# Loads of x in smaller pieces with a limit on those in flight, a shorter chain to the band matrix, and a new order of work

## The chip, the cores and the metric

The kernel runs on one core of a Trainium2 chip. The metric is the device time of one execution in microseconds. Its engines are named as the profile does: PE (TensorE, matrix products; PEld is its loading of weights), ACT (ScalarE), DVE (VectorE), POOL (GpSimd) and SP (SyncE). PE writes its results to PSUM, eight banks of 512 float32 columns on 128 partitions. ACT and DVE move results from PSUM to SBUF. POOL and SP issue transfers (DMAs) between DRAM and SBUF here, which sixteen DMA engines carry out.

## The reference

The input x has 8 batches of 4224 tokens with 192 channels. A causal convolution over 7 tokens comes first, with one softmax-normalised filter for each of 8 heads of 24 channels. A token-mixing layer follows:

```
w   = softmax(weight, axis=-1)                        # [8 heads, 7 taps]
y   = sum over k of w[h, k] * x_pad[b, s + k, h, :]   # x_pad: 6 zero rows ahead of x
W   = (y @ w_q) @ (y @ w_k).T / sqrt(64)              # [b, 4224, 4224]
out = relu(W @ y) @ w_out
```

The kernel never forms W. It computes the 192 x 192 matrix G = y.T y per batch, makes M = w_k.T G from it, and then relu((y w_q) M / 8) w_out.

## The kernel before

Tokens are cut into 35 chunks of 122. Each is held in SBUF as 128 rows, its own 122 and the 6 ahead of it, so that a convolution is one matmul per head with a 128 x 128 band matrix, `BAND`. x is loaded by POOL, cast to bf16 on the way, into `XW`, which has room for all 8 batches. A load therefore never waits for space.

Per batch the work is: convolution of groups of chunks (`gen_conv`, L636), evacuated to `Y` (L671); transposes of Y (L395/L396 through a helper, and L726), evacuated to `YTL` and `YTH` (L698, L733); the product with w_q (L751, L755) to `WQT` (L771); the Gram matrix (L787); the small product M (`gen_mix_weights`); then, a batch later, the mixing matmuls (L878, L890), a relu (L907 on ACT, L908 on DVE), the product with w_out (L935, and L391/L392 through the helper `halves`), evacuation to `OUT` (L970) and a store by SP (L978).

A DMA from DRAM to `XW` carries rows of 192 channels, 384 bytes each once they are bf16. Batch 0 is loaded in four groups of 9 or 8 chunks; every later batch in two, of 18 and 17. The first chunk of a batch (no rows ahead of it) and the last (a short one) have small DMAs of their own. The DMAs of a group share a semaphore, and the group's convolutions wait for it.

Ahead of the first convolution stands a chain: an identity (POOL), a step matrix made from it (DVE L435), its transpose (PE, ACT L445), the softmax on small tiles (DVE L461 to L494 with one exponential on ACT, L482), matmuls that spread the taps (`spread`, L508), and two evacuations that make `BAND` (L527), one on ACT and one on DVE. DVE also clears several tiles in that time, in program order with the chain: `WQH`, `WKT`, `WKB`, `YTH`, `WQT`, `MBD` (L417, L419, L420, L411, L410, L422).

Nothing in the source fixes the order of the rest. Every step is an `Op` with assumed costs, what it needs, what it must follow (`after`, order only) and a turn. `Planner.plan` (L143) places the ops one by one: on each engine, of the ops that could start, the one with the lowest turn goes first. The turns come from the table `TURNS`, one number per op in the order in which the ops are made. PE ops have a mode (64 output rows from 128 input rows, or the other way); a change of mode costs `SWITCH` in the plan and `STAY` is added to the turn of an op that would change it. `HOLD` is how many ns PE may wait for an op of the mode it is in. The plan also chooses ACT or DVE for most evacuations, and PSUM banks. `Program` then gives each engine its list in that order, with semaphore waits where one engine needs another. The engines execute their lists in order.

Of the kernel before, what the change touches and what calls it, by code (L numbers as in the profile page):

```python
# [13 lines left out]
    int(t) / 1000  # L14
    for t in """
# [56 lines left out]
class Op:  # L72


    n = 0
# [28 lines left out]
class Planner:  # L104
# [6 lines left out]
    STAY = 0.865  # L111

    HOLD = 1
# [166 lines left out]
def bass_lightweight_conv__then__hypermixer_token_mlp_kernel(  # L280
# [25 lines left out]
    t = 0  # L306
# [67 lines left out]
    def bank(i, n=1):  # L374
        return PS[:, i * 512 : (i + n) * 512]

    def add(*a, dma=None, kind=None, **k):
        op = Op(*a, **k)
        op.dma = dma
        op.kind = kind  # L380
        op.vt = TURNS[len(planner.ops)]
        return planner.add(op)
# [11 lines left out]
    def turn_halves(e, out, in_, identity):  # L394
# [34 lines left out]
        1250,  # L429
# [28 lines left out]
        200, needs=[ident], vt=-8.92)  # L458
# [44 lines left out]


    bands = []
    for q0, engine in ((0, "ACT"), (4, "DVE")):

        def spread(e, op, q0=q0):  # L508
            last = None
            for q in range(q0, q0 + 4):  # L510
                last = halves(
                    e,
                    bank(op.bank)[:, (q - q0) * 128 : (q - q0 + 1) * 128],
                    STEPT[0:112, 112 - 16 * q : 240 - 16 * q],
                    TAPS[0:112, :, :].rearrange("p i h -> p (i h)"),
                    start=q == q0,
                    stop=q == q0 + 3,
                    skip_group_check=True,
                )
            return last  # L520

        fill = add("PE", spread, 260, needs=[taps, stept], banks=1, vt=-7 + 0.1 * q0)

        def band(e, op, q0=q0, fill=fill):
            dst = BAND[:, :, 16 * q0 : 16 * q0 + 64]
            src = bank(fill.bank).rearrange("p (j h) -> p h j", h=H)
            return e.copy(dst, src) if op.engine == "ACT" else e.tensor_copy(dst, src)  # L527

        bands.append(add(engine, band, 550, drains=fill, vt=-6.9))
# [3 lines left out]
    at = [5000.0]  # L533

    def gen_load(b, gi):
        sem = semaphore(f"s_x{b}_{gi}")
# [4 lines left out]
        if cs[0] == 0:  # L541
            parts.append((XW[KC - 1 : 128, b, 0, :], bass.AP(x_t, base, [[D, CW], [1, D]])))
        n = len(full)
        parts.append(
            (
                XW[:, b, full[0] : full[0] + n, :],
                bass.AP(x_t, base + (CW * full[0] - KC + 1) * D, [[D, 128], [CW * D, n], [1, D]]),
            )
        )
# [9 lines left out]
        at[0] += len(cs) * 260.0  # L559
        load[b, gi] = []  # L560
        for k, part in enumerate(parts):
            first = (b, gi) == (0, 0) and part[0].shape[1] > 1 and len(part[0].shape) == 3
            op = add(
# [3 lines left out]
                needs=[zero_x] if cs[-1] == NCC - 1 else [],  # L567
                after=[] if first else [ident],
                dma=(f"x{b}_{gi}", sem, 16),
                vt=-10 if first else -4 + b + gi * 0.1 + 0.02 * k,  # L570
            )
            op.tail = 1500.0
            op.lands = at[0]
# [485 lines left out]
```

## Time and profile before

| | us |
|---|---|
| median of 3 runs | 177.69 |
| lowest, highest | 177.29, 178.58 |
| the profiled execution | 177.53 |
| its span, first to last instruction | 175.7 |

In the page, x3226 is a number of instructions; a share is of the span. The parts that matter besides the lines shown with the prediction:

```profile
## 2 busy tenths in 40 slices
PE   0289799888999999899989979999999999999990
...
POOL 7999452524230000000000000000000000000000
...
DMA  3999999999999999999999999067283045987787
GB/s 30 162 189 186 205 191 193 191 196 277 193 279 194 286 309 268 343 250 243 304 264 282 237 194 348 24 244 297 103 343 127 4 175 216 356 347 309 265 303 262
```

Each slice is 4.4 us long; a digit is the busy share in tenths. The DMA row is full up to slice 24, some 105 us: in that time the loads of x run, with the stores of results among them from slice 8 on. After it only stores are left. In slices 2 to 8 loads run alone, at some 190 GB/s, counted in bytes that land.

```profile
q0 software_dynamic: 36128, 13.61, 65.1%
q1 hardware_dynamic: 12000, 26.31, 40.9%
...
out_dram<-out_sb SPq DMA_DIRECT2D x28, 768.0 KB, 5.1
xw<-in_x_dram POOLq DMA_DIRECT2D x7, 816.0 KB, 33.2
```

q0 are the loads of x that POOL issues (packets, MB, share of 16 engines' time); q1 the weights and the stores that SP issues. The last two lines give, for a group of DMAs, the KB of each and the median time from issue to landing. The seven large loads of 17 chunks take 33.2 us because they are issued long before their turn comes in the queue.

### The profile page before, as it was taken

The numbers are of one execution on the slowest core, as the hardware profiler recorded it, in microseconds if no ns is written. First come the engines' busy times: TensorE is split into PE (matmuls) and PEld (weight loads), VectorE is DVE, ScalarE is ACT, GpSimd is POOL, SyncE is SP. The second block draws the span as 40 slices with busy tenths as digits, with TensorE's granted clock in tenths as the row PEclk, the third lists the DMA queues.
The fourth block names the chain that finished last, engine by engine and source line by source line (L and its number), as shares of the span: only waits on it lengthen the run. The fifth ranks groups of instructions, "written<-read, shape, count | busy, mean of one in ns | idle before, by whom it ended". The sixth has DMA issues, their size and how long they took to land.

```text
span 175.7 us, 7099 instructions
## 1 busy us (share of the span) xinstructions
PE 157.1 (89%) x3226; PEld 121.7 (69%) x3226; DVE 118.0 (67%) x216; ACT 123.5 (70%) x206; POOL 30.3 (17%) x39
## 2 busy tenths in 40 slices
PE   0289799888999999899989979999999999999990
PEld 0179666776787787668778766878767777877550
DVE  6556587765766677586787738689688675765740
ACT  3243677597787948668648747888888896698980
POOL 7999452524230000000000000000000000000000
PEclk9999999999999999999999999999999999999995
DMA  3999999999999999999999999067283045987787
GB/s 30 162 189 186 205 191 193 191 196 277 193 279 194 286 309 268 343 250 243 304 264 282 237 194 348 24 244 297 103 343 127 4 175 216 356 347 309 265 303 262
DMA packets 48157, 40.36 MB, mean 230 GB/s; under 512 B 37632, under 2 KB 40960, under 8 KB 48128
## 3 DMA queue, kind: packets, MB, share of 16 engines
q0 software_dynamic: 36128, 13.61, 65.1%
q1 hardware_dynamic: 12000, 26.31, 40.9%
q8 instruction: 25, 0.41, 0.9%
q14 instruction: 4, 0.03, 0.1%
HBM read 27.56 MB, written 25.95 MB: 305 GB/s over the span
## 4 chain that ended last, share of the span: by engine, by line
PE 88%; issue 4%; DVE 3%; ACT 2%
PE ps L391 25%; PE ps L787 14%; PE ps L935 8%; PE ps L392 7%; PE ps L395 6%; PE ps L726 6%; PE ps L878 5%; PE ps L751 4%; PE ps L890 4%; PE ps L755 4%; PE ps L396 3%; ACT rt L907 1%; ACT out_sb L970 1%; DVE band L527 0%; DVE xw L416 0%
## 5 line engine op out<-in xcount | busy, mean ns | idle before, releaser
L970 ACT COPY out_sb<-ps 128x768 f32<-128x768 f32 (+1 forms) x46 | 34.7, 768 | 15.1 <-PE ps L392 11.3
L671 ACT CAST y<-ps 122x816 bf16<-122x816 f32 (+3 forms) x46 | 35.7, 791 | 13.2 <-PE ps L392 12.8
L907 ACT ACTIVATE rt<-ps 128x1024 bf16<-128x1024 f32 (+3 forms) x44 | 34.1, 800 | 6.4 <-PE ps L878 4.5
L787 PE MATMUL ps<-y 122*64 122x192 bf16 (+4 forms) x840 | 33.8, 222 | 2.2 <-issue 2.2
L970 DVE COPY out_sb<-ps 128x768 f32<-128x768 f32 (+1 forms) x26 | 21.6, 840 | 19.7 <-PE ps L392 18.5
L392 PE MATMUL ps<-wol,rt 128*64 128x192 bf16 x264 | 33.9, 255 | 1.0 <-issue 1.0
L787 PEld LDWEIGHTS ps<-y 122*64 122x64 bf16 (+1 forms) x840 | 31.1, 112 | 4.9 <-issue 2.8
L565 POOL DMA_DIRECT2D xw<-in_x_dram x34 | 29.9, 893 | 22.3 <-issue 21.5
L391 PE MATMUL ps<-wol,rt 128*64 128x192 bf16 x264 | 33.7, 255 | 0.0
L391 PE MATMUL ps<-xw,band 128*64 128x432 bf16 (+3 forms) x144 | 31.8, 335 | 1.5 <-DVE band L527 0.9
L392 PE MATMUL ps<-xw,band 128*64 128x432 bf16 (+3 forms) x144 | 32.1, 337 | 1.1 <-issue 1.1
L391 PEld LDWEIGHTS ps<-wol,rt 128*64 128x64 bf16 x264 | 24.1, 138 | 8.1 <-issue 2.0
L908 DVE TENSOR_SCALAR rt<-ps 128x512 bf16<-128x512 f32 (+3 forms) x36 | 23.6, 674 | 8.2 <-PE ps L878 7.6
L671 DVE CAST y<-ps 122x864 bf16<-122x864 f32 (+3 forms) x26 | 23.6, 912 | 8.0 <-PE ps L392 7.5
L698 DVE COPY ytl<-ps 128x976 bf16<-128x976 bf16 (+1 forms) x40 | 23.0, 591 | 3.9 <-PE ps L396 3.3
L392 PEld LDWEIGHTS ps<-wol,rt 128*64 128x64 bf16 x264 | 24.1, 138 | 1.2 <-issue 1.2
L396 PE MATMUL ps<-ident,y 122*64 122x122 bf16 x280 | 21.1, 219 | 0.0
L395 PE MATMUL ps<-ident,y 122*64 122x122 bf16 x280 | 21.0, 219 | 0.0
L935 PE MATMUL ps<-woh,rt 64*128 64x192 bf16 x264 | 20.4, 250 | 0.2 <-ACT rt L907 0.2
L395 PEld LDWEIGHTS ps<-ident,y 122*64 122x64 bf16 x280 | 18.1, 112 | 2.0 <-issue 0.5
L726 PE MATMUL ps<-ident,y 122*64 122x122 bf16 (+1 forms) x344 | 17.1, 220 | 1.3 <-DVE y L671 0.7
L396 PEld LDWEIGHTS ps<-ident,y 122*64 122x64 bf16 x280 | 17.7, 112 | 0.0
(95 smaller groups left out, 218.8 us busy)
## 6 DMA issues: line engine op xcount, KB each, us to landing
out_dram<-out_sb SPq DMA_DIRECT2D x28, 768.0 KB, 5.1
xw<-in_x_dram POOLq DMA_DIRECT2D x7, 816.0 KB, 33.2
xw<-in_x_dram POOLq DMA_DIRECT2D x7, 768.0 KB, 33.7
out_dram<-out_sb SPq DMA_DIRECT2D x8, 384.0 KB, 3.3
xw<-in_x_dram POOLq DMA_DIRECT2D x2, 432.0 KB, 8.3
out_dram<-out_sb SPq DMA_DIRECT2D x8, 96.0 KB, 4.3
xw<-in_x_dram POOLq DMA_DIRECT2D x1, 384.0 KB, 5.2
xw<-in_x_dram POOLq DMA_DIRECT2D x8, 45.8 KB, 25.0
```

Source lines behind the costliest of these rows:

```text
L391: e.matmul(out[0:64], lhsT[:, 0:64], rhs, **k)
L392: return e.matmul(out[64:128], lhsT[:, 64:128], rhs, **k)
L395: e.transpose(out[0:64], in_[:, 0:64], identity)
L396: return e.transpose(out[64:128], in_[:, 64:128], identity)
L565: lambda e, op, part=part: e.dma_start(*part),
L671: return e.copy(dst, src) if op.engine == "ACT" else e.tensor_copy(dst, src)
L726: last = e.transpose(ps[64 * i : 64 * i + HI, o : o + w], Y[0:w, yb, c, LO:D], IDENT[0:w, 0:w])
L787: mm = e.matmul(bank(GB)[p : p + 64, o : o + z - r], Y[0:w, yb, c, r : r + 64], Y[0:w, yb, c, r:z], start=st, stop=end, skip_group_check=True,
L907: return e.activation(dst, src(), AF.Relu)
L908: return e.tensor_scalar(dst, src(), 0.0, None, op0=ALU.max)
L935: last = e.matmul(bank(op.bank + a)[:, o : o + D], RT[64 * a : 64 * a + HI, slot, 2, i:n:nt], WOH[64 * a : 64 * a + HI, :], start=i == q, ...
L970: return e.copy(dst, src) if op.engine == "ACT" else e.tensor_copy(dst, src)
```

## The change

Loads: for b >= 1 the full chunks of a group go in four DMAs of 4 or 5 chunks each instead of one. Every DMA has a semaphore of its own. Each load of b >= 1, small ones too, waits until the third of the large loads ahead of it has landed. The assumed landing times of batch 0 are changed, and the assumed tail of a later load is 3200 ns.

```diff
+    big_loads = []
+    LANDS = [6000.0, 9900.0, 12300.0, 13900.0]
...
+        pieces = 4 if b else 1
+        for k in range(pieces):
+            some = full[len(full) * k // pieces : len(full) * (k + 1) // pieces]
+            parts.append(
+                (
+                    XW[:, b, some[0] : some[0] + len(some), :],
+                    bass.AP(x_t, base + (CW * some[0] - KC + 1) * D, [[D, 128], [CW * D, len(some)], [1, D]]),
+                )
             )
...
+            gate = big_loads[-3:][:1] if b else []
             op = add(
                 "POOL",
                 lambda e, op, part=part: e.dma_start(*part),
                 900,
-                needs=[zero_x] if cs[-1] == NCC - 1 else [],
+                needs=[*([zero_x] if cs[-1] == NCC - 1 else []), *gate],
                 after=[] if first else [ident],
-                dma=(f"x{b}_{gi}", sem, 16),
+                dma=(f"x{b}_{gi}_{k}", semaphore(f"s_x{b}_{gi}_{k}"), 16),
...
-            op.tail = 1500.0
-            op.lands = at[0]
+            op.tail = 1500.0 if b == 0 else 3200.0
+            op.lands = LANDS[gi] if b == 0 else 0.0
+            if len(part[0].shape) == 3:
+                big_loads.append(op)
```

Start: six clears are ordered behind the last step of the softmax (`taps`), `own` gets a later turn, and the band is spread and copied in four parts, two on ACT and two on DVE, instead of two.

```diff
+    for zero in (zero_w, zero_q, zero_yt, *zero_k, zero_m):
+        zero.after.append(taps)
...
-    for q0, engine in ((0, "ACT"), (4, "DVE")):
+    for q0, engine in ((0, "ACT"), (2, "DVE"), (4, "ACT"), (6, "DVE")):
...
-            dst = BAND[:, :, 16 * q0 : 16 * q0 + 64]
-            src = bank(fill.bank).rearrange("p (j h) -> p h j", h=H)
+            dst = BAND[:, :, 16 * q0 : 16 * q0 + 32]
+            src = bank(fill.bank)[:, 0 : 32 * H].rearrange("p (j h) -> p h j", h=H)
```

Order: all numbers of `TURNS` are new (two more ops for the band and 42 more for the loads are among them), and the planner's constants change.

```diff
-    STAY = 0.865
-    HOLD = 1
+    STAY = 0.909457
+    HOLD = 46.721672
```

The built orders show what comes of it. PE has the same matmuls in a new order. In the new one the convolutions of a batch's two halves stand further from each other in the early batches, and those of batch 7 stand earlier, after 2320 and 2344 of PE's 3226 matmuls instead of 2518 and 2448 for the second and first half. A convolution's first matmul waits for two to four semaphores of x instead of one. POOL has 76 loads instead of 34. On DVE the six clears stand between the taps and the first band copy. ACT has 38 large output copies instead of 43, DVE 26 instead of 21.

More of the change, by code (lines that the diff above doesn't have):

```diff
@@ L13 @@
 TURNS = [
-    int(t) / 1000
+    int(t) / 1e6
     for t in """
[50 rows of a table removed]
[84 rows of a table added]
 """.split()
@@ L428, in bass_lightweight_conv__then__hypermixer_token_mlp_kernel @@
         ),
-        1250,
+        700,
         needs=[one],
@@ L457, in bass_lightweight_conv__then__hypermixer_token_mlp_kernel @@
         lambda e, op: e.tensor_reduce(OWN[:, :], IDENT[:, :].rearrange("p (k i) -> p i k", i=16), AX.X, ALU.add),
-        200, needs=[ident], vt=-8.92)
+        200, needs=[ident], vt=-7.83)
     mx = add("DVE", lambda e, op: e.tensor_reduce(WMX[:, :], WT_F[:, :, :], AX.X, ALU.max), 150, needs=[load_w], vt=-8)
@@ L502, in bass_lightweight_conv__then__hypermixer_token_mlp_kernel @@
     taps.needs.append(own)
+    for zero in (zero_w, zero_q, zero_yt, *zero_k, zero_m):
+        zero.after.append(taps)
     bands = []
-    for q0, engine in ((0, "ACT"), (4, "DVE")):
+    for q0, engine in ((0, "ACT"), (2, "DVE"), (4, "ACT"), (6, "DVE")):
         def spread(e, op, q0=q0):
             last = None
-            for q in range(q0, q0 + 4):
+            for q in range(q0, q0 + 2):
                 last = halves(
@@ L516, in spread @@
                     start=q == q0,
-                    stop=q == q0 + 3,
+                    stop=q == q0 + 1,
                     skip_group_check=True,
@@ L520, in spread @@
             return last
-        fill = add("PE", spread, 260, needs=[taps, stept], banks=1, vt=-7 + 0.1 * q0)
+        fill = add("PE", spread, 200, needs=[taps, stept], banks=1, vt=-7 + 0.1 * q0)
         def band(e, op, q0=q0, fill=fill):
-            dst = BAND[:, :, 16 * q0 : 16 * q0 + 64]
-            src = bank(fill.bank).rearrange("p (j h) -> p h j", h=H)
+            dst = BAND[:, :, 16 * q0 : 16 * q0 + 32]
+            src = bank(fill.bank)[:, 0 : 32 * H].rearrange("p (j h) -> p h j", h=H)
             return e.copy(dst, src) if op.engine == "ACT" else e.tensor_copy(dst, src)
-        bands.append(add(engine, band, 550, drains=fill, vt=-6.9))
+        bands.append(add(engine, band, 340, drains=fill, vt=-6.9))
     load = {}
-    at = [5000.0]
+    big_loads = []
+    LANDS = [6000.0, 9900.0, 12300.0, 13900.0]
     def gen_load(b, gi):
-        sem = semaphore(f"s_x{b}_{gi}")
         cs = groups_of(b)[gi]
@@ L542, in gen_load @@
             parts.append((XW[KC - 1 : 128, b, 0, :], bass.AP(x_t, base, [[D, CW], [1, D]])))
[L543 to L547, printed above, removed]
+        pieces = 4 if b else 1
[6 more added lines that the diff above has]
+                )
             )
-        )
         if cs[-1] == NCC - 1:
@@ L557, in gen_load @@
             )
-        at[0] += len(cs) * 260.0
         load[b, gi] = []
```

134 rows, old and new, of the table TURNS are left out of this document.

## The prediction

> **What bounds the kernel now.** I read the engine shares first, then PE in stretches, then each place where PE stands still.
>
> ```profile
> span 175.7 us, 7099 instructions
> ...
> PE 157.1 (89%) x3226; PEld 121.7 (69%) x3226; DVE 118.0 (67%) x216; ACT 123.5 (70%) x206; POOL 30.3 (17%) x39
> ...
> q8 instruction: 25, 0.41, 0.9%
> ```
>
> PE is busy 157.1 of 175.7 us, ACT and DVE 70 and 67%: PE is the bound, and a gain must come from the 18.6 us in which it is idle. The stretches (stretch, its length, PE busy and its matmuls, then PEld, DVE, ACT, POOL, the clock, the DMA share) place them:
>
> ```profile
> 80.00:100.00 20.00, 19.41 (x436) 15.65 (x435) 14.29 (x26) 13.78 (x26) 0.00 (x0) 1.00 1.39 257
> ...
> 120.00:140.00 20.00, 20.00 (x434) 15.44 (x430) 15.57 (x24) 16.81 (x28) 0.00 (x0) 1.00 0.43 165
> ```
>
> From 120 to 140 us PE never rests, and the stretch to 160 us reads 20.00 too. While the loads of x run (the last lands at 106.0 us; the DMA share is 1.3 to 1.6) it does. The other idle times are the start, 8.7 us until the first convolution, and the end, 4.8 us of evacuation and store after the last matmul. The timeline of PE shows all stops over 0.3 us after 12 us:
>
> ```profile
> 20.48 0.35 PE L787 MATMUL ps<-y 122*64 122x192 bf16 x5 [1.28 <-issue]
> ...
> 33.15 0.19 PE L726 MATMUL ps<-ident,y 76*64 76x76 bf16 x1 [0.50 <-issue]
> ...
> 40.15 0.33 PE L392 MATMUL ps<-xw,band 128*64 128x408 bf16 x1 [1.07 <-issue]
> ...
> 70.96 0.30 PE L787 MATMUL ps<-y 122*64 122x64 bf16 x4 [0.90 <-issue]
> ...
> 90.19 0.34 PE L391 MATMUL ps<-xw,band 128*64 128x432 bf16 x1 [0.59 <-issue]
> ...
> 103.09 0.30 PE L392 MATMUL ps<-wol,rt 128*64 128x192 bf16 x1 [0.99 <-issue]
> ```
>
> Together 5.33 us, and "issue" means that PE waited for nothing shown; two stand between the two halves of one L391/L392 pair, where the program has no wait. The DMA packets name the cause. Queue q8 moves 25 packets of 16 KB. Before each stop one of them ends 1.4 to 1.5 us before PE goes on: 18.96, 31.72, 38.66, 69.60, 88.72 and 101.67 us. Counted in PE's records, the first instructions after the stops are numbers 449, 961, 1217, 2497, 3265 and 3777: steps of whole multiples of 256, and 16 KB / 256 is 64 bytes. PE runs out of program. From the passing of one such boundary to the start of the next packet took 3.3 to 4.5 us for the 14 packets up to 103 us (mean 3.8), then 0 to 2.7 us (mean 1.3). With 0.95 us for the packet and 1.42 us after it a page arrives some 6.2 us after the boundary; PE uses one up in about 6. So through the whole load phase PE runs on the edge of its program supply. Stores show the same delay: 768 KB landed in 7 to 10 us during the loads and in 3.4 to 5.2 us after them.
>
> **The change, part by part.** Sums are against the profiled execution, 177.53 us: span 175.7 and 1.8 around it. The median of the runs, 177.69, lies 0.16 higher.
>
> *Pieces and gate.* Each half-batch load of b >= 1 (16 or 17 chunks) becomes four of 4 or 5 chunks, each issued when the third large load ahead has landed: at most three, some 600 KB, in flight, where the old kernel has up to seven large loads (816 KB) issued and not landed. On POOL behind the waiting instruction stand only later loads. POOL executes 42 more issues; the trace has 0.55 us for a one-chunk load, 0.98 for 7 chunks and 1.28 for 17, so about 0.85 us each and some 65 us in all on an engine that is otherwise idle. DVE does not feel them: its 128x976 copy takes 660 ns both while POOL issues (10 to 53 us) and after (661).
> What it buys is the wait of 3.8 us before each program packet. A piece has 4 x 128 / 16 = 32 rows per DMA engine. A gated piece is not at once there: POOL's issue (0.85) and the start of its packets come first, in which the two others are served, 1.03 us each at the 190 GB/s of the store-free slices. So a packet that arrives should find about one piece, 1 to 2 us, ahead of it. Page latency is then 1.5 + 0.95 + 1.42, about 4 us, under the 6 that PE needs, and the stops go. Bounds: 0 (the wait stays) and -6 (the six stops, and small ones at the other eight boundaries). By rate: 1653 matmuls between 20.5 and 103.1 us are 20.0 per us; at the 21.2 of 103 to 160 us they take 4.6 us less. I take -5.0, between the rate and the stops. What is late next is PE's own work.
>
> *The start.*
>
> ```profile
> 3.42 0.12 DVE L435 COPY step<-ident 128x128 bf16<-128x128 bf16 x1
> ...
> 4.70 0.15 DVE L461 TENSOR_REDUCE wmx<-wt_f 128x8 f32<-128x56 f32 x1
> ...
> 7.93 0.69 DVE L527 CAST band<-ps 128x512 bf16<-128x512 f32 x1 [1.16 <-PE ps L392]
> ```
>
> Six memsets leave the chain: three start from 3.02 on, ahead of the step copy (3.42), three from 4.28 on, ahead of wmx (4.70); 0.8 us in all. The identity is there at 2.70, DVE free at 2.94, so the step copy starts near 3.04 (-0.4) and wmx at 3.9; the weights landed at 3.75, so they just do not bind. The taps end at 5.96 instead of 6.76, PE starts at 6.02. The six memsets (0.82) now stand between taps and bands on DVE, 6.03 to 6.85; its first band's fill is done at 6.65, so 0.2 us of them show. A quarter of the band (256 columns) costs about 0.42 us on DVE (0.69 for 512, 0.29 for a 128-column cast from PSUM) and 0.38 on ACT: bands end near 7.7 instead of 8.62. First convolution -0.9; the first x landed by 6.8, so it does not bind. It carries through if later loads are in time: the fourth group's landing, 15.1 us, is 2.3 ahead of its convolution. Between -0.2 and -1.2; I take -0.9.
>
> *The order.* PE's instructions are the same; the built orders have 97 changes between 64-row and 128-row matmuls instead of 107. At the end of the trace one such change delays the next matmul by 0.05 to 0.09 us: 10 x 0.07 = -0.7 (0 to -1.4). Waits on x grow from 18 to 52, each extra one an instruction of 51 ns on PE's sequencer; in the trace those lie beside the running matmul nearly everywhere, so +0.3 of a possible 1.7. Evacuations shift from ACT to DVE (five output copies, 0.80 against 0.96 us, and five 512-column relus), with three casts the other way: both stay near 70%, +0. The tail keeps its form: eight 384 KB stores and a last one of 96 KB, 0.
>
> Sum: -5.0 - 0.9 - 0.7 + 0.3 = -6.3, so 171.2 in a profiled execution and **171.4 us** as the median.
>
> **Rivals.**
>
> *The fetch waits as before.* Its wait was the same, 3.3 to 4.5 us, with seven large loads queued (18 us) and with the last two (97 us), so it may hang on there being any load at all. The sum without -5.0 is 176.4 us. Against it: a piece holds 32 rows per engine, the old loads 136, and gated pieces leave gaps. The Trainium skill says so outright ("DMA: Bandwidth & Descriptors", section "Queues, rings and completion order"): each engine goes round the queues packet by packet, so a shorter backlog in one queue would not shorten the wait of another. The trace's constant wait agrees with that; whether the packets of a small piece are shorter no run shows. Chance 0.14.
>
> *The loads starve.* The weights' 28 KB took 2.95 us from issue to landing; with 1.03 us of data a piece takes 4.0 us, so three make 147 GB/s, 23% under the 190 of before. Under stores the loads made only 100 GB/s even with a full queue, so there the limit of three costs little. Need and landing: in the new order the first half of batch 1 comes after 310 matmuls instead of 308, so it is needed at 23.5 - 1.28 - 0.9 = 21.3 us, and by my chain (issues at 11.4, 13.2, 15.1 and 16.4) lands at 20; the second half of batch 5 comes after 1628 matmuls, which the trace reached at 90.7, so it is due near 85.5 (stops up to there and the start taken off) and landed at 77.1 before; batch 7 comes after 2320, at 124.0, so it is due near 118 and landed by 106.0. Counted from 21.3, the old landing of its first group, the loads may be 14% slower. At 23% throughout, batch 7 comes at 125.5, 7.6 us late: 179 us, slower than before. It decides from 21% on (6.3 us late). The Trainium skill speaks for this ("DMA: Bandwidth & Descriptors", section "Bandwidth"): DMAs should be batched to 1 MiB or more. Chance 0.10.
>
> *The new order stalls PE elsewhere.* 303 PE instructions wait instead of 293, and convolutions move. From 160 to 165 us PE idles 0.18 us in 5 on evacuations; at that density over 140 us it is +5.0: 176.4. Against it, 120 to 160 us shows none. Chance 0.10.
>
> **Numbers.** The forecast has 0.62, its own range 169 to 174.5; a better order still, under 169, 0.04. A change under 1%, 1.8 us, can't be told from none in such runs, so "faster" ends at 175.9. The two rivals at 176.4 count mostly as the same; their milder halves (some stops left) still as faster: faster 0.75, same 0.15, slower 0.10. Range 169.0 to 177.0: it leaves out starved loads and part of the lucky side.
>
> **What would show it.** Right: no "issue" stops on PE between 18 and 105 us, program packets starting within 2 us of their boundary, stores landing sooner during the loads, a first convolution near 7.9 us, PE near 21 matmuls per us throughout, batch 7 landed before 118 us. Wrong: PE waiting for an x load in front of a convolution, stops at multiples of 256 instructions still there, or PE idle behind evacuations in the stretches that were full.

## The result, and the profile after

| | before | after |
|---|---|---|
| median, us | 178.09 (4 runs, 177.29 to 178.58) | 197.44 (4 runs, 196.07 to 198.78) |
| the profiled execution, us | 177.53 | 197.81 |
| its span, us | 175.7 | 196.1 |
| large loads all landed, us | 106.0 | 140.9 |

The ratio is 1.109 (95% interval 1.100 to 1.118): slower, where 171.4 us was forecast. The ratios below leave out executions well above the rest, among them the profiled ones of e9 and e13 (823.5 and 223.7 us), whose traces are not read; where that matters, the whole spread is given.

The chain that ended last, by engine, in the kernel before:

```profile
PE 88%; issue 4%; DVE 3%; ACT 2%
```

The page of the changed kernel, its shares, its clock, the same chain by engine and by line, and the loads' row:

```profile
span 196.1 us, 7150 instructions
...
PE 164.2 (84%) x3226; PEld 127.6 (65%) x3226; DVE 123.7 (63%) x219; ACT 120.6 (62%) x205; POOL 55.9 (29%) x81
...
PEclk9999999999969999999589999999559999999998
...
DMA 62%; PE 22%; POOL 8%; issue 4%; ACT 1%; DVE 0%; POOLq 0%; DVEq 0%
DMA xw<-in_x_dram 60%; POOL xw L606 8%; PE ps L425 6%; PE ps L978 3%; PE ps L830 3%; DMA out_dram<-out_sb 2%; PE ps L921 2%; PE ps L429 2%; PE ps L426 1%; PE ps L933 1%; PE ps L794 1%; PE ps L798 1%; PE ps L769 1%; ACT rt L950 1%; PE ps L430 0%
...
xw<-in_x_dram POOLq DMA_DIRECT2D x49, 192.0 KB, 5.5
```

PE was the bound before, with 88% of the chain; now 60% of it is loads of x, and another 8% their issue. PE is idle for 32 us instead of 18.6, and its clock, full until the tail before, falls to half three times. POOL's waits say which loads (line waited for, us in total, times, longest):

```profile
POOL xw L606 <- DMA xw<-in_x_dram: 80.2, 42, 5.2
```

42 of the 70 loads of b >= 1 had to wait, 80 us in all, of the 127 us between the first of these loads (issued at 11.6 us) and the last (138.9). All stops of PE over 0.4 us after 12 us, from its timeline:

```profile
14.87 0.24 PE L429 MATMUL ps<-ident,y 122*64 122x122 bf16 x1 [0.85 <-ACT y L714]
...
22.85 0.34 PE L425 MATMUL ps<-xw,band 128*64 128x432 bf16 x1 [0.62 <-DVE ytl L741]
...
36.88 0.34 PE L425 MATMUL ps<-xw,band 128*64 128x432 bf16 x1 [0.45 <-DMA xw<-in_x_dram]
...
54.16 0.34 PE L425 MATMUL ps<-xw,band 128*64 128x432 bf16 x1 [4.79 <-DMA xw<-in_x_dram]
...
75.75 0.32 PE L978 MATMUL ps<-woh,rt 64*128 64x192 bf16 x3 [0.48 <-issue]
...
93.21 0.54 PE L425 MATMUL ps<-xw,band 128*64 128x432 bf16 x1 [3.63 <-DMA xw<-in_x_dram]
...
141.07 0.52 PE L425 MATMUL ps<-xw,band 128*64 128x408 bf16 x1 [7.61 <-DMA xw<-in_x_dram]
```

The six "issue" stops of 5.33 us have shrunk to one of 0.48 (75.75): that part came as forecast. In their place stand four stops for x of 0.45 + 4.79 + 3.63 + 7.61 = 16.5 us. Each long one also costs after it. In the same view by stretches as in the prediction (the clock is the third number from the end), beside the two long stops at 54 and 141 us:

```profile
44.00:49.00 5.00, 4.94 (x113) 4.00 (x109) 2.78 (x6) 4.32 (x8) 2.08 (x4) 1.00 1.17 175
...
54.70:58.00 3.30, 3.30 (x52) 2.90 (x49) 1.98 (x3) 1.76 (x2) 1.02 (x2) 0.50 1.29 211
...
141.10:146.70 5.60, 5.60 (x69) 4.35 (x71) 2.25 (x3) 1.72 (x3) 0.00 (x0) 0.50 0.02 3
146.90:152.00 5.10, 5.10 (x119) 4.38 (x114) 4.26 (x7) 2.91 (x7) 0.00 (x0) 1.00 0.00 0
```

PE is busy throughout, at a clock of 0.50: 69 matmuls in 5.6 us, then 119 in 5.1. By the clock's records the half clock was granted from 54.66 us for 3.4 us, from 92.20 for 6.8 and from 136.57 for 10.2. Of these 20.5 us, 5.5 lie inside the second and the third stop; PE worked at half clock for 3.4, 5.8 and 5.7 us, 15.0 together, worth up to 7.5 us. How much the loads slowed is plainest between 14 and 32 us, where no store runs (queue q0: packets, MB, and the time of its packets as a share of the 16 engines' own). Before, then after:

```profile
q0 software_dynamic: 8217, 3.12, 144.4%
```

```profile
q0 software_dynamic: 5862, 2.17, 112.2%
```

In 18 us that is 173 GB/s before and 120 after: the loads run at 70% of their old rate. Three pieces of 192 KB, 590,000 bytes, over the 4.8 us that one took from issue to landing there give 123 GB/s, about that rate. Beside stores the loads brought 92 GB/s from 45 to 95 us, against 107; from the landing of batch 3 to that of batch 7 they took 79.7 us (61.2 to 140.9) instead of 59.8 (46.2 to 106.0).

The start, on DVE:

```profile
2.97 0.26 DVE L469 COPY step<-ident 128x128 bf16<-128x128 bf16 x1
...
3.74 0.48 DVE L495 TENSOR_REDUCE wmx<-wt_f 128x8 f32<-128x56 f32 x1
...
7.08 0.69 DVE L564 CAST band<-ps 128x256 bf16<-128x256 f32 x2
```

The step copy starts at 2.97 instead of 3.42, the band copies at 7.08 instead of 7.93, and the first convolution at 7.92 instead of 8.76.

Up: 16.5 us of stops, up to 7.5 of half clock, and two stops behind evacuations (0.85 and 0.62). Down: 4.85 of program stops, 0.84 of start. That is +19.8 of the 20.4 us between the spans, the half clock counted at its most.

### The profile page after: what moved, and what is told of

It reads as the page before. It is cut to its first block, busy times and chain, and to the rows that moved or that the text cites. A ratio compares the mean times of both kernels' runs of the same rounds, so it can differ in the third digit from the quotient of the medians.

```text
span 196.1 us, 7150 instructions
## 1 busy us (share of the span) xinstructions
PE 164.2 (84%) x3226; PEld 127.6 (65%) x3226; DVE 123.7 (63%) x219; ACT 120.6 (62%) x205; POOL 55.9 (29%) x81
## 4 chain that ended last, share of the span: by engine, by line
DMA 62%; PE 22%; POOL 8%; issue 4%; ACT 1%; DVE 0%; POOLq 0%; DVEq 0%
DMA xw<-in_x_dram 60%; POOL xw L606 8%; PE ps L425 6%; PE ps L978 3%; PE ps L830 3%; DMA out_dram<-out_sb 2%; PE ps L921 2%; PE ps L429 2%; PE ps L426 1%; PE ps L933 1%; PE ps L794 1%; PE ps L798 1%; PE ps L769 1%; ACT rt L950 1%; PE ps L430 0%
## 5 line engine op out<-in xcount | busy, mean ns | idle before, releaser
L606 POOL DMA_DIRECT2D xw<-in_x_dram x76 | 55.4, 734 | 83.1 <-DMA xw<-in_x_dram 80.2
L425 PE MATMUL ps<-xw,band 128*64 128x408 bf16 (+3 forms) x144 | 34.1, 358 | 17.9 <-DMA xw<-in_x_dram 16.5
L1013 DVE COPY out_sb<-ps 128x768 f32<-128x768 f32 (+1 forms) x32 | 26.8, 844 | 21.1 <-PE ps L426 13.9
L1013 ACT COPY out_sb<-ps 128x768 f32<-128x768 f32 (+1 forms) x40 | 30.7, 776 | 14.8 <-PE ps L426 14.1
L950 ACT ACTIVATE rt<-ps 128x1024 bf16<-128x1024 f32 (+3 forms) x42 | 31.4, 768 | 7.7 <-PE ps L921 6.8
L830 PE MATMUL ps<-y 122*64 122x64 bf16 (+3 forms) x840 | 34.3, 228 | 0.7 <-DVE y L714 0.7
L426 PE MATMUL ps<-xw,band 128*64 128x408 bf16 (+3 forms) x144 | 34.3, 359 | 0.0
L425 PEld LDWEIGHTS ps<-xw,band 128*64 128x64 bf16 x144 | 15.0, 122 | 22.3 <-issue 19.5
L951 DVE TENSOR_SCALAR rt<-ps 128x512 bf16<-128x512 f32 (+3 forms) x38 | 27.2, 729 | 2.6 <-PE ps L921 1.7
L429 PEld LDWEIGHTS ps<-ident,y 122*64 122x64 bf16 x280 | 19.4, 117 | 3.0 <-ACT y L714 1.1
L814 ACT CAST wqt<-ps 128x512 bf16<-128x512 f32 (+1 forms) x26 | 13.1, 508 | 12.7 <-PE ps L798 12.5
```

The lines of the kernel that those rows point to most:

```text
L425: e.matmul(out[0:64], lhsT[:, 0:64], rhs, **k)
L426: return e.matmul(out[64:128], lhsT[:, 64:128], rhs, **k)
L429: e.transpose(out[0:64], in_[:, 0:64], identity)
L606: lambda e, op, part=part: e.dma_start(*part),
L830: mm = e.matmul(bank(GB)[p : p + 64, o : o + z - r], Y[0:w, yb, c, r : r + 64], Y[0:w, yb, c, r:z], start=st, stop=end, skip_group_check=True,
L950: return e.activation(dst, src(), AF.Relu)
```

## The experiments

Three theories of the lost time stood against each other: G, the limit of three starves the loads; P, small pieces are slow in themselves; O, the new order is at fault. For the wait of the program packets it was B (it follows the loads in flight) against R (it is the same whenever loads run). The diffs show the lines that matter, with `...` for what is left out between them. Except where said, the order of every engine's other work is left untouched. "L" is the time at which the last packet of x ends and "W" the mean wait of a program packet while loads run, both read from the packets of the trace.

**e1: the changed kernel without the limit.** The order is planned as before, and the waits dropped afterwards:

```diff
     planner.plan()
+    for ops in load.values():
+        for op in ops:
+            op.needs = [x for x in op.needs if x not in op.gate] + []
```

> The changed kernel, its order and its small pieces, but no load waits for another. Theory G (the limit of three starves the loads): everything is landed near 106 us instead of 140.9, PE's stops on x (16.5 us) and the clock of 0.5 behind them go; whether the program stops come back then decides between some 171 (they stay away) and 176.4 us (they are back, my sum without its -5.0). Theory P (small pieces are slow however many are in flight): landed near 140 us as with the limit, and 190 us or more. Theory O (the new order asks for x too early or stalls by itself): landed near 106 us, and still 183 us or more.

178.70 us, ratio 1.007 [1.004, 1.010]; L 105.8, W 3.8 us. Three of PE's stops on its timeline:

```profile
20.82 1.04 PE L831 MATMUL ps<-y 122*64 122x64 bf16 x30 [1.71 <-issue]
...
46.15 0.48 PE L831 MATMUL ps<-y 122*64 122x64 bf16 x10 [0.47 <-issue]
...
97.20 0.52 PE L979 MATMUL ps<-woh,rt 64*128 64x192 bf16 x8 [0.66 <-issue]
```

No stop waits for x, and the program stops are back. The limit alone made 18.7 us (197.4 to 178.7). The run is 2.3 us above the 176.4 that theory G had for program stops that come back; G does not explain these 2.3.

**e2: the changed kernel's order and start with the old whole loads.**

```diff
-            some = full[len(full) * k // pieces : len(full) * (k + 1) // pieces]
+            some = full if k == 0 else []
```

> The changed kernel's order and start, with the loads as they were before: one DMA for each half batch, nothing waited for. Theory G: the order and the start alone, so -0.9 -0.7 and the stops of the program as before: 176 us, within 1.5. Theory O: 183 us or more, with PE idle on x or behind evacuations though all of x is landed by 106 us. Theory P: as G, and at least 10 us below the run with small pieces and no limit.

177.53 us, ratio 0.999 [0.996, 1.002]; W 3.7. G again, at the very end of its band (174.5 to 177.5): the start and the order together bring nothing.

**e3: the kernel before with its loads in pieces, no waits.** A load op becomes four, each with a semaphore of its own, after the plan (`if 0`: no wait is added):

```diff
+        cuts = [n * k // 4 for k in range(4 + 1)] if whole else [0, 1]
...
+                part = (dst[:, c0:c1, :], bass.AP(src.tensor, src.offset + c0 * CW * D, [list(d0), [CW * D, c1 - c0], list(d2)]))
...
+            one.needs = list(op.needs) + (big[-1:][:1] if 0 else [])
```

> The kernel before with nothing but its half-batch loads of b >= 1 cut in four pieces, without any wait between loads. Theories G and O: between 176 and 179 us, loads landed by 110 us, program packets starting 3 to 4.5 us after their boundary as before. Theory P: loads landed near 140 us and 185 us or more. If the wait of the program packets hangs on the size of a DMA and not on the backlog, the stops of 5.3 us go and it takes 172 to 174 us.

177.16 us, ratio 0.997 [0.994, 0.999]; L 106.0, W 3.8. P falls: the pieces land as the whole loads do, and the wait of the packets does not hang on the size of a DMA.

**e4, e5, e6: the old order with pieces and a limit of three, four, five.** As e3, with this line for a limit of three, and 4 or 5 in it for the others:

```diff
+            one.needs = list(op.needs) + (big[-3:][:1] if 3 else [])
```

> The kernel before with its loads in pieces and the limit of three, its own order and start. Theory G: the same landings as in the changed kernel (batch 3 at 54 and 61 us, batch 7 at 134 and 141), against needs at 47.7, 54.3 and 129.7, 134.0 us in this order: PE stops for 6 to 9 us in all on x, the clock falls behind these stops, the program stops (5.3 us) go: 181 to 190 us. Theory O (the order is what fails): 172 to 178 us.

> As the old order with pieces and the limit of three, with a limit of four. Theory G, sized by the runs so far: a piece in flight takes some 4.5 us however few are in flight, so four give one piece every 1.15 us instead of 1.5 (1.0 without a limit); batch 2's second half lands near 37 us against a need at 37.8, PE stops on x for 0 to 2 us. Theory B (the wait of a program packet follows the number of loads in flight): 3 us on average instead of 3.8, the program stops gone: 172 to 176 us. Theory R (the wait is the same as soon as the loads' queue is hardly ever empty): 3.5 us or more and the stops stay: 176 to 179 us.

> As before with a limit of five: five pieces of 4.5 us give 0.9 us each, under the 1.0 of the data, so the landings are those without a limit while no stores run. Theory B: a wait of 3.3 to 3.7 us, part of the stops gone, 173 to 176 us. Theory R: 3.8 us, 176.5 to 178 us, the same as without a limit.

| limit | GB/s, 14 to 32 us | flight, us | L | W | time, us | ratio |
|---|---|---|---|---|---|---|
| 3 (e4) | 125 | 5.5 | 140.2 | 2.6 | 188.36 | 1.057 [1.049, 1.065] |
| 4 (e5) | 140 | 6.7 | 122.9 | 3.3 | 181.39 | 1.023 [1.019, 1.027] |
| 5 (e6) | 152 | 7.5 | 113.2 | 3.7 | 177.22 | 0.995 [0.992, 0.999] |
| none (e3) | 172 | 21.4 | 106.0 | 3.8 | 177.16 | 0.997 [0.994, 0.999] |

(Flight is the page's median from issue to landing of a 192 KB load.) Step by step both things happen that were forecast: with fewer loads in flight the packets wait less, theory B, and the loads come later, theory G. The second is the dearer one at every step. My expectation for five, no loss of rate without stores, was wrong (152 against 172 GB/s), and its time is the one that theory R gave (all ten executions of e6: 175.5 to 181.8 us); four was dearer than expected. In e4, PE's stops are of both kinds, 9.4 us on x and, against the expectation, still 4.3 of program stops over 0.4 us. Three of them:

```profile
43.48 0.52 PE L391 MATMUL ps<-xw,band 128*64 128x408 bf16 x1 [3.79 <-DMA xw<-in_x_dram]
...
81.55 0.33 PE L391 MATMUL ps<-xw,band 128*64 128x408 bf16 x1 [2.62 <-DMA xw<-in_x_dram]
...
132.41 0.69 PE L788 MATMUL ps<-y 122*64 122x192 bf16 x17 [2.46 <-issue]
```

The last is a program stop again: its packet waited 6.7 us, beside stores, for loads that without a limit would have been done by then. Theory O falls as the main cause, since the old order loses 10.9 us to the same limit; but the changed kernel, with the new order, is 9.1 us slower still.

**e7, e8: both orders without the loads of batches 1 to 7.**

```diff
-                        XW[:, b, c0 : c0 + n, GRP * h : GRP * h + GRP],
+                        XW[:, 0, c0 : c0 + n, GRP * h : GRP * h + GRP],
```

> The kernel before in its own order, with the loads of batches 1 to 7 left out: their convolutions read batch 0's x. It prices all that the loads cost PE. If the stops in the load phase come from program packets that wait for loads, packets start within 2 us of their boundary, no stop over 0.3 us is left between 18 and 105 us and it takes 171 to 173.5 us. If they have another cause: 176 us or more.

> The changed kernel in its own order and with its start, with the loads of batches 1 to 7 and their waits left out: the same for the new order. By the prediction's terms for the start and the order (-0.9, -0.7, and no extra waits) it is 1.6 us under the same run of the old order: 169.5 to 172 us. Theory O' (the new order costs PE what its start gains): the same as the old order within 0.5 us, or above it.

170.30 us in the old order, below the 171 to 173.5 that was expected, ratio 0.960 [0.955, 0.964]; 172.26 in the new one, 0.973 [0.966, 0.979]. W is 0.5 and 1.0 us. The stretches of e7:

```profile
60.00:80.00 20.00, 20.00 (x436) 15.66 (x433) 13.86 (x24) 15.02 (x27) 0.00 (x0) 1.00 0.48 185
80.00:100.00 20.00, 20.00 (x461) 16.24 (x457) 16.30 (x29) 13.05 (x23) 0.00 (x0) 1.00 0.40 155
```

PE never rests, 461 matmuls instead of 436 in the second: with no loads the program stops are gone, and 7.1 us (177.42 to 170.30) bounds what curing them could bring, since this run leaves out all that the loads cost. Theory O' holds: the new order, with its faster start, is 2 us slower by itself (1.0 by the spans of the two profiled executions). Part of it is seen in e8's timeline of PE:

```profile
14.89 0.24 PE L429 MATMUL ps<-ident,y 122*64 122x122 bf16 x1 [0.67 <-ACT y L714]
```

PE waits 0.67 us for ACT to move Y out. The first convolution is 0.85 us ahead of e7's there, the fourth group's (17.3 against 17.5 us) only 0.2: the start's gain is gone by then.

**e9, e10: the old order, unlimited up to batch 3, and a limit of three or four from batch 4 on.** As e4, with this line for three, and a 4 in it for four:

```diff
+            one.needs = list(op.needs) + (big[-3:][:1] if op.b >= 4 else [])
```

> The kernel before with pieces, unlimited up to batch 3 and with the limit of three from batch 4 on. In the run with the limit throughout a batch took some 20 us under stores; from batch 3's landing at 45.5 us that gives the second halves of batches 4 to 7 at 66, 86, 105 and 125 us, against needs at 75.9, 93.2, 119.2 and 134.0, so PE waits for no x. Theory B (the wait of a program packet follows the loads in flight): waits near 2 us from 50 us on, the stops behind it go (2.5 us of 5.3 there): 173 to 175.5 us. Theory R (the same wait as long as the loads run): 177 to 178.5 us. If limited loads beside stores bring the long packet waits of 5 to 7 us that the runs with three and four showed from 107 us on: 176 to 179 us, with stops between 100 and 125 us.

> The same with four in flight from batch 4 on: waits near 3 us instead of 3.8, no stop on x. Theory B: 174 to 176.5 us. Theory R: 177 to 178.5 us.

Neither is a gain that can be relied on. e10's twelve executions spread from 174.38 to 179.16 us around 177.64, against 177.59 for the kernel before; the five that can be read of e9 from 175.15 to 180.26. The ratios, 0.987 [0.983, 0.992] for e10 and 0.988 [0.981, 0.995] for e9, are of the lower part of those spreads. In the trace of e10 W is 3.8 us: four in flight beside stores bring nothing to the program packets, so B was too hopeful there.

**e11: one part of the start in the old order.** The six clears go behind the taps on DVE, `own` behind the exponential:

```diff
     planner.plan()
+    moved = [op for op in planner.order if op in (zero_w, zero_q, zero_yt, *zero_k, zero_m)]
...
+        if op is taps:
+            late += moved
```

> The kernel before with one part of the change's start alone: the six clears moved behind the taps on DVE, and own moved behind the exponential; nothing else is touched. The first convolution comes 0.5 to 0.8 us sooner (8.76 before). If what is gained ahead of the first convolution reaches the end, 176.6 to 177.0 us on 177.4; if PE then only waits longer for x or for its program, 177.2 to 177.6 us.

176.58 us, ratio 0.994 [0.991, 0.996]. The first convolution comes at 7.86 us instead of 8.76, matmul 171 of PE at 16.3 instead of 17.4, the last matmul ends 0.8 us sooner: in the old order the start's gain reaches the end.

**e12: e9 and e11 together.**

> Both of the above together: their gains add up if each is real, 172.5 to 175 us by theory B; 176.5 to 177.5 us by theory R.

179.37 us (all twelve from 176.9 to 183.0), ratio 1.004 [1.000, 1.009]: the expectation was wrong. A batch took 22 us under the limit, not 20, and PE stops on x again, in front of batch 7:

```profile
134.91 0.52 PE L391 MATMUL ps<-xw,band 128*64 128x408 bf16 x1 [3.52 <-DMA xw<-in_x_dram]
```

**e13, e14: the new order with a limit of five; and with two pieces for a half batch and a limit of three.** In e13 the waits are exchanged after the plan:

```diff
+            op.gate, op.wide = gate, big_loads[-5:][:1] if b else []
...
+            op.needs = [x for x in op.needs if x not in op.gate] + op.wide
```

In e14 a piece takes two quarters, every other piece is left out, and the limit counts the larger ones:

```diff
-            some = full[len(full) * k // pieces : len(full) * (k + 1) // pieces]
+            some = full[len(full) * k // pieces : len(full) * (k + 2) // pieces] if b else full
...
+            op.needs += large[-3:][:1]
```

> The changed kernel, its order, start and pieces, with a limit of five instead of three. If the bytes in flight are what starves the loads (five pieces, 980 KB, against 590 KB), the stops on x and the half clock go: 176 to 180 us. If it is the waiting on POOL, however many are in flight, 185 us or more.

> The changed kernel with two pieces for each half batch instead of four, and still a limit of three: half as many waits on POOL, twice the bytes in flight (some 1.2 MB). By the bytes in flight: 176 to 180 us, program packets waiting near 3.8 us again. By the number of loads in flight: 185 us or more.

e13 took 178.30 us, ratio 1.003 [1.000, 1.006], and e14 177.34 us, 0.994 [0.990, 0.998]; e14's executions spread from 175.1 to 179.9, around the time of before. In e14 there are still three in flight, but of 384 KB: 168 GB/s between 14 and 32 us, L 113.3 and W 3.6 us. It is the bytes in flight that starve the loads, not their number nor the waits on POOL.

**e15: e3 and e11 together**, the two parts that did no harm.

> The kernel before with the clears behind the taps and its loads in pieces without a limit: the two parts that did no harm alone (ratios 0.9937 and 0.9966). If they add up 0.990, some 175.9 us; if the second is noise, 176.6 us.

176.55 us, ratio 0.994 [0.992, 0.997]. The clears are the whole gain; the pieces add nothing. This, or e11, is the best kernel of the study, 1 us under the one before.

## Why the prediction was wrong

**The step that failed is "Pieces and gate".** The sum counted there only what a shorter backlog buys, -5.0, and put the price of the limit, later loads of x, at nothing; the limit cost 18.7 us (e1). That price stood in the rival "The loads starve", with the right mark of it (PE waiting for x in front of a convolution), but at a chance of 0.10, because its size was wrong three times. A piece was put at 4.0 us of flight, made up of 2.95 us of the weights' small DMA and 1.03 of data; it took 4.8 without stores, and the loads ran 30% slower where 23% was counted. (And the 23% were taken from the 190 GB/s of the slices without stores, where x does not run alone: between 14 and 32 us all queues together, weights among them, made 194 GB/s and x 173, against which the forecast 147 are 15% less.) "So there the limit of three costs little", said of the time under stores, was an argument from 100 GB/s with a full queue; a batch took some 20 us there instead of 15. And landings add up: batch 7 came at 140.9 us, (140.9 - 21.3) / (106.0 - 21.3) = 1.41 times as late as before, against the 14% that the order could bear and the 21% from which the rival was to decide. The rival's own 23% was already beyond both; by its own condition it was not a case of 0.10. e1, e4 to e6, e13 and e14 settle the cause.

**The price of a stop** was counted as its length. Behind the three long ones PE ran at half clock for 15.0 us, worth up to 7.5, which no term and no rival had.

**"The wait goes" was right in direction.** W fell from 3.7 to 2.2 us and the stops from 5.33 to 0.48, for the -5.0 that was taken. How much of that is owed to the long stops on x, in which PE uses no program, is not shown: in e4, at a W of 2.6, 4.3 us of program stops are left. e7 gives 7.1 us as the ceiling. The rival "The fetch waits as before" fell with it: by the Trainium skill's turn-taking between queues ("DMA: Bandwidth & Descriptors", section "Queues, rings and completion order") a shorter backlog would not have shortened that wait, and the measured 2.6, 3.3, 3.7 and 3.8 us for three, four, five and unlimited loads (e4, e5, e6, e3) say that it does. The Trainium skill states the turns; that the backlog does not matter was drawn from them. The Trainium skill's rule of DMAs of 1 MiB or more ("DMA: Bandwidth & Descriptors", section "Bandwidth") pointed the right way: with 590 KB in flight the loads starved, with 1.2 MB (e14) hardly. That these 1.2 MB were three DMAs of 384 KB, and that unlimited loads of 192 KB (e3) lose nothing, says that it is the sum in flight that counts here and not the size of one DMA.

**The start** was sized right, 7.92 us for 7.9. "It carries through if later loads are in time" failed: not a load but an evacuation of Y stopped PE at 14.2 us (0.67 to 0.85 us) in the new order. In the old order (e11) it does carry through, 1.0 us.

**The order** was to bring -0.7 by ten mode changes less. Taken with the start it brought nothing (e2) or +2 us (e8 against e7), so by itself, with the start's 0.84 us taken off, it cost from 0.9 to 2.8 us. Where the rest beyond the stop at 14.2 us lies was not traced. Under the limit it cost more: after the last long stop the changed kernel still has 906 matmuls to do and the old order, whose first convolutions of batch 7 come after 2448, 778; 128 matmuls at 21.2 per us are 6.0 us, and the 5.7 us at half clock behind that stop, worth up to 2.9, have no counterpart in e4 at that place. Together up to 8.9 us, of the 9.1 measured between the two.

## What to carry to other kernels

A limit on transfers in flight is a limit on their rate: bytes in flight over the time from issue to landing. Measure that time with the loads themselves, beside whatever runs then, and compare the last landing with the need of it before counting the gain. A stop of the matrix engine is to be counted with the half clock behind it, and what is gained ahead of the first matmul is a gain only if the next wait does not take it.

## What the runs showed of the hardware

A program page for PE waits for loads that are in flight at the time, but only up to a point: 0.5 us with no loads (e7), then 2.6, 3.3 and 3.7 us with three, four and five of 192 KB in the old order (2.2 with three in the new one), and 3.8 with all of them queued. Limited loads that last into the stores can also do worse: 6.7 us in e4 and e5, each with a stop of PE behind it (2.46 and 2.64 us).

The half clock comes in steps of 3.41 us and behind stops shorter than one: after 2.09 us at 29 us in e4, 2.07 in e5 and 1.78 in e14, while e4's stops of 2.62 and 2.46 left the clock full. In each of the five traces with more than one stretch of half clock, the tail counted (the changed kernel, e4, e5, e12, e14), these start whole multiples of 3.41 us apart; in the changed kernel those at 92.20 and 136.57 start 11 and 24 steps after that at 54.66. Ahead of the tail, PE's idle time inside one step of this grid tells nearly always what the next step gets: 2.07 to 3.41 us were followed by half clock, 1.88 or less were not, except for the 1.78 of e14. e4's stops of 2.62 and 2.46 fell across two steps, with 1.71 and 1.88 in the fuller one. A step already at half clock was followed by another after only 1.0 and 1.1 us of idle (changed kernel, from 92.20 and 139.99). So where a stop falls in the grid bears on what it costs; idle time is not the whole rule, since in the tails 1.0 to 1.5 us were enough. The Trainium skill ("TensorE: Matmul & The Clock Gate", section "Part 1: The HAM clock gate (the "warmup" mystery)") has the half clock after at least one idle window of about 3.4 us; the length of the step agrees with these runs, the idle time that is needed does not.
